# Two layers of cached attention and FFN: most of TensorE's program becomes a repeated block of four units

## The chip, the cores and the metric

The kernel runs on one core of a Trainium2 chip. Its engines are TensorE (PE: matmuls; PEld: its weight loads), VectorE (DVE), ScalarE (ACT), GpSimd (POOL) and SyncE (SP), which here issues every DMA. Sixteen DMA engines move the data. Each engine runs its own program in order and waits on semaphores for the others. The metric is device microseconds of one execution; times are medians of several runs. A trace of one execution, taken by the hardware profiler, gives a profile.

## What is computed

Four rows of x (batch 4, one position, width 512) go twice through an attention layer over a cache of 8192 keys and values and then through a gated FFN:

```python
def _A_ref(x, k_cache, v_cache, wq, wo):      # Hq 32 heads, Hkv 8 groups, Dh 128
    q = (x @ wq).reshape(B, Sq, Hq, Dh).transpose(0, 2, 1, 3)
    scores = einsum("bhqd,bhkd->bhqk", q, repeat(k_cache, 4)) * Dh ** -0.5
    o = einsum("bhqk,bhkd->bhqd", softmax(scores), repeat(v_cache, 4))
    return o.transpose(0, 2, 1, 3).reshape(B, Sq, Hq * Dh) @ wo
def _B_ref(x, w_gate, w_up, w_down):
    return (silu(x @ w_gate) * (x @ w_up)) @ w_down
x = x + _A_ref(_layernorm(x), ...);  x = x + _B_ref(_layernorm(x), ...)   # and both once more
```

Both layers use the same weights and the same caches. K and V are 64 MB each in bf16, read once per layer.

## The kernel before

**Units.** A unit is one pair of a key group g (8) and a batch row b (4): 2 MB of K and 2 MB of V, 32 units a layer. `unit_order` runs through them, in layer 1 beginning with the last three of layer 0, whose K and V are kept in memory and not loaded again. In this text "the 31st unit" is the 31st in a layer's order.

**Slots.** SBUF has eight slots of 2 MB for K and V (`NSLOT`). `pump` (L316) issues loads on SP in a fixed order (`items`: K of a unit, then V of the unit before it, in between and at the end the weights), each into a free slot that `fit` and `max` choose. A load is issued when `finished` (L363) has put a slot back: after the last scores of a K, after the last product of a V. At the end of a layer the weights of the FFN take slots 6 and 7.

**The work of a unit.** DVE transposes each of the eight blocks of a K in place (`turn`, L401). PE computes the scores of a block with four matmuls (`scores`, L421), with the queries that POOL has laid out in `zq` (`place_q`, L412). When all eight are done, the steps of the softmax follow: DVE's maximum over the partitions (`max_p`, L427), PE's transpose of it and DVE's second maximum (`max_t`, L431 and L434), ACT's copy (L437), PE's spreading of it and ACT's exponentials (`exps`, L443, L447, L449, L451), DVE's transpose of the probabilities (`turn_p`, L454), PE's sums and their reciprocal (`total`, L457, L459). Then PE multiplies them with V (`values`, 16 matmuls, L517), ACT and DVE add up the parts (L526, L531), PE sums rows (L536) and DVE scales into `oT` (L556). For the last two units of a layer V is taken in 8 blocks of 8 small matmuls (`block_last`, L549).

**Order.** The program of every engine is written out in full by Python, in one order. DVE's transposes are emitted first; the blocks that use them lag behind by at most `LAG` = 2.0 us of estimated work (`drain`), and the steps of softmax (`line`) and of the sums (`after`) are put between blocks as their estimated gaps run down (`advance`, L382). Each operation waits for what it reads and for the readers of what it writes (`_Sync`); a wait is a constant value of a semaphore. TensorE's program is 9,792 matmuls and weight loads long.

**Projection.** When the four units of a group are done, `out_proj` (L575) multiplies the group's outputs with its part of `wo`: 16 small matmuls that bring `oT` into place (L581), a copy to `o4` on DVE (L584), 16 matmuls (L587) and DVE's addition to x (L572). So there is one after every fourth unit, and `oT` has two buffers.

**Between layers.** `center` (L597 to L610) and `deviation` (L613) are the layer norm, `ffn` (L647) takes gate and up (L659), SiLU (L664 to L671) and down (L676), `qproj` (L621) the queries of the next layer.

## Time and profile before

| what | value |
|---|---|
| runs | 655.31 us median of 3 (654.31 to 655.44) |
| the profiled execution | 655.51 us, its span 653.7 us |
| mean granted TensorE clock | 0.824 |
| HBM read | 273.88 MB, 419 GB/s over the span |
| DVE transposes of K, L401, x488 | 322.4 us, 686 ns each; idle before them 121.8 us, ended by the load of K |
| PE scores, L421, x2048 | 346.2 us, 314 ns each |
| PE products with V, L517, x960 | 68.5 us, 409 ns each |
| PE projections, L581 and L587, x256 each | 6.6 and 9.2 us |
| DVE addition to x, L572, x21 | 3.6 us; idle before it 15.3 us, 11.2 of it for PE's L587 |
| loads of K, x60, and of V, x58, 2 MB | 30.0 and 33.8 us from issue to landing |

The first part of the page gives each engine's busy time and its share of the span. The slices show forty equal parts of the span: a 9 in the DMA row means that the sixteen DMA engines were busy for nine tenths of that slice or more. The rows on queues tell whose packets the DMA engines moved: q1 carries the kernel's loads, q8 and q14 instructions of the engines' programs. The chain is followed back from the last instruction to whatever released each step. A line of a timeline has the start and the length in us, the engine, the line of the program, the operation with what it writes and reads, the count of merged instructions, and in brackets the engine's idle time before and what ended it. Under all this the trace keeps one record for each DMA packet: its queue, size, start and duration. A load ends on each DMA engine with a packet of 4 bytes, the completion mark.

### The profile page before, as it was taken

The numbers are of one execution on the slowest core, as the hardware profiler recorded it, in microseconds if no ns is written. First come the engines' busy times: TensorE is split into PE (matmuls) and PEld (weight loads), VectorE is DVE, ScalarE is ACT, GpSimd is POOL, SyncE is SP. The second block draws the span as 40 slices with busy tenths as digits, with TensorE's granted clock in tenths as the row PEclk, the third lists the DMA queues.
The fourth block names the chain that finished last, engine by engine and source line by source line (L and its number), as shares of the span: only waits on it lengthen the run. The fifth ranks groups of instructions, "written<-read, shape, count | busy, mean of one in ns | idle before, by whom it ended". The sixth has DMA issues, their size and how long they took to land.

```text
span 653.7 us, 11807 instructions
## 1 busy us (share of the span) xinstructions
PE 500.5 (77%) x4896; PEld 319.2 (49%) x4896; DVE 446.1 (68%) x1079; ACT 116.4 (18%) x391; POOL 19.3 (3%) x73
## 2 busy tenths in 40 slices
PE   1766787977777877787876988887688787786886
PEld 1544444544444544544555655554354454443456
DVE  2556676776776777776752399996677677676682
ACT  0021121221221221221220212221122122121120
POOL 0000000000000000000000000000000000000000
PEclk9897788777978778789685989997978887797895
DMA  9999999999999999999999999999999999999996
GB/s 368 428 425 423 438 429 427 432 431 429 430 431 429 430 430 432 430 432 428 427 416 375 398 411 431 430 428 429 430 428 429 433 430 430 432 427 429 432 420 239
DMA packets 24085, 274.64 MB, mean 420 GB/s; under 512 B 2392, under 2 KB 2400, under 8 KB 7904
## 3 DMA queue, kind: packets, MB, share of 16 engines
q1 hardware_dynamic: 24032, 273.89, 98.9%
q8 instruction: 38, 0.62, 0.3%
q14 instruction: 15, 0.12, 0.0%
HBM read 273.88 MB, written 0.00 MB: 419 GB/s over the span
## 4 chain that ended last, share of the span: by engine, by line
DMA 66%; DVE 17%; PE 13%; SPq 3%; issue 1%; ACT 0%; POOL 0%; DVEq 0%; POOLq 0%
DMA kvf<-in_A_k_cache_dram 63%; DVE kvf L401 11%; PE ps L421 8%; DVE acc L531 3%; DMA kvf<-in_B_w_down_dram 3%; SPq L93 2%; PE ps L517 1%; DVE one L427 1%; DVE pT L454 1%; PE ps L587 1%; DVE m L434 1%; PE ps L625 1%; PE ps L457 0%; PE ps L676 0%; PE ps L549 0%
## 5 line engine op out<-in xcount | busy, mean ns | idle before, releaser
L401 DVE STREAM_TRANSPOSE kvf<-kvf 128x512 f32<-128x512 f32 x488 | 322.4, 686 | 121.8 <-DMA kvf<-in_A_k_cache_dram 121.8
L421 PE MATMUL ps<-kvf,zq 128*128 128x256 bf16 x2048 | 346.2, 314 | 18.2 <-DVE kvf L401 15.7
L421 PEld LDWEIGHTS ps<-kvf,zq 128*128 128x128 bf16 x2048 | 211.3, 115 | 89.8 <-DVE kvf L401 40.4
L437 ACT ACTIVATE pb<-m 1x128 f32<-1x128 f32 x64 | 19.7, 308 | 453.5 <-DVE m L434 453.5
L431 PE MATMUL ps<-identf,one 128*1 128x128 f32 x64 | 18.3, 286 | 68.3 <-DVE one L427 68.3
L517 PE MATMUL ps<-kvf,pT 128*16 128x512 bf16 x960 | 68.5, 409 | 0.9 <-DVE rl L459 0.9
L531 DVE SCALAR_TENSOR_TENSOR acc<-ps,own,acc 128x128 f32<-128x128 f32 x180 | 63.1, 351 | 6.5 <-ACT acc L526 1.9
L431 PEld LDWEIGHTS ps<-identf,one 128*1 128x1 f32 x64 | 5.1, 80 | 99.4 <-DVE one L427 93.2
L536 PE MATMUL ps<-head,acc 128*128 128x4 f32 x120 | 26.4, 290 | 17.9 <-DVE acc L531 17.7
L536 PEld LDWEIGHTS ps<-head,acc 128*128 128x128 f32 x120 | 22.8, 237 | 34.2 <-DVE acc L531 33.6
L443 PE MATMUL ps<-one,pb 1*128 1x1 f32 x128 | 27.8, 284 | 14.1 <-ACT pb L437 13.8
L443 PEld LDWEIGHTS ps<-one,pb 1*128 1x128 f32 x128 | 22.4, 217 | 32.8 <-ACT pb L437 29.1
L449 ACT ACTIVATE pb<-ps,one,rstd 128x256 bf16<-128x256 f32 x64 | 36.2, 565 | 2.1
L412 POOL TENSOR_TENSOR zq<-scr,quad 128x64 bf16<-128x64 bf16 x62 | 18.2, 293 | 608.1 <-PE ps L421 569.4
L517 PEld LDWEIGHTS ps<-kvf,pT 128*16 128x16 bf16 x960 | 19.3, 91 | 32.8 <-issue 21.2
L427 DVE TENSOR_REDUCE one<-ps 128x1 f32<-128x256 f32 x64 | 25.6, 399 | 13.1 <-PE ps L421 12.7
L454 DVE STREAM_TRANSPOSE pT<-pb 128x256 bf16<-128x256 bf16 x64 | 25.9, 405 | 1.9 <-ACT pb L449 1.9
L457 PEld LDWEIGHTS ps<-rsm,one 128*128 128x128 f32 x128 | 24.5, 237 | 3.0 <-ACT rsm L451 0.9
L457 PE MATMUL ps<-rsm,one 128*128 128x4 f32 x128 | 21.6, 239 | 0.0
L447 ACT ACTIVATE one<-ps,rstd 128x1 f32<-128x1 f32 x64 | 16.7, 261 | 25.8 <-PE ps L443 25.8
L526 ACT ACTIVATE acc<-ps,own 128x128 f32<-128x128 f32 x60 | 20.6, 343 | 0.0
L434 DVE TENSOR_REDUCE m<-ps 1x4 f32<-1x128 f32 x64 | 15.6, 244 | 6.5 <-PE ps L431 6.5
(66 smaller groups left out, 165.9 us busy)
## 6 DMA issues: line engine op xcount, KB each, us to landing
kvf<-in_A_k_cache_dram SPq DMA_DIRECT2D x60, 2048.0 KB, 30.0
kvf<-in_A_v_cache_dram SPq DMA_DIRECT2D x58, 2048.0 KB, 33.8
wq_sb<-in_A_wq_dram SPq DMA_DIRECT2D x4, 1024.0 KB, 7.6
wo_sb<-in_A_wo_dram SPq DMA_DIRECT2D x4, 1024.0 KB, 34.5
kvf<-in_A_v_cache_dram SPq DMA_DIRECT2D x8, 512.0 KB, 19.3
kvf<-in_B_w_gate_dram SPq DMA_DIRECT2D x2, 1792.0 KB, 23.2
kvf<-in_B_w_down_dram SPq DMA_DIRECT2D x4, 768.0 KB, 16.0
kvf<-in_A_v_cache_dram SPq DMA_DIRECT2D x2, 1024.0 KB, 7.0
```

The lines of the kernel that those rows point to most:

```text
L401: T.op("dve", lambda e: e.transpose(w, w), reads=[f"s{s}.{q}"], writes=[f"s{s}.{q}"])
L421: T.op("pe", lambda e: e.matmul(bank(bk)[:, 0:SW], lhsT=zq[:, c, z0:z0 + P], rhs=w[:, :, c // 2, :, c % 2], start=(q == 0 and c == 0), sto ...
L427: T.op("dve", lambda e: e.tensor_reduce(mx[:], bank(bk)[:, 0:SW], AX.X, ALU.max), reads=[f"pb{bk}"], writes=["mx"])
L431: T.op("pe", lambda e: e.matmul(bank(STEP)[0:1, 0:P], lhsT=mx[:], rhs=identf[:], is_transpose=True, start=True, stop=True), reads=["mx", " ...
L434: T.op("dve", lambda e: e.tensor_reduce(m4[:], bank(STEP)[0:1, 0:P].rearrange("p (x h) -> p h x", h=REP), AX.X, ALU.max, negate=True), rea ...
L443: T.op("pe", lambda e: e.matmul(bank(STEP)[:, 0:1], lhsT=mrow, rhs=onesf[0:1, :], start=True, stop=True), reads=["pb", "onesf"], writes=[f ...
L449: T.op("act", lambda e: e.activation(pb[:], bank(bk)[:, 0:SW], ACTF.Exp, bias=nm[:], scale=by, accum_out=rs[:]), reads=[f"pb{bk}", "nm", " ...
L454: T.op("dve", lambda e: e.transpose(pT[:, turn_of[u], :], pb[:]), reads=["pb"], writes=[f"pT{turn_of[u]}"])
L457: T.op("pe", lambda e: e.matmul(bank(TOT)[:, 0:REP], lhsT=ones, rhs=rsm[:], start=True, stop=True), reads=["rsm", "onesf"], writes=[f"pb{T ...
L517: T.op("pe", lambda e: e.matmul(bank(bk)[j * QB:j * QB + NV * REP, :], lhsT=pT[:, turn_of[u], c0:c0 + NV * REP], rhs=v[:, t, NV * i:NV * ( ...
L531: T.op("dve", lambda e: e.scalar_tensor_tensor(acc[:], bank(bk)[:, k * Dh:(k + 1) * Dh], own[:, k:k + 1], acc[:], op0=ALU.mult, op1=ALU.ad ...
L536: T.op("pe", lambda e: e.matmul(bank(LNB)[:, 0:REP], lhsT=acc[:], rhs=head[:], start=True, stop=True), reads=["acc", "head"], writes=[f"pb ...
```

## The change

- **A tape for TensorE.** Matmuls are no longer issued at once. `T.pe` records them, with their waits, on a tape, and `play` issues them at the end of the build. The other engines' programs are built as before.
- **A repeated block.** `roll` cuts the tape at the heads of the units, looks in each layer for the longest run in which the operations of four units equal those of the next four (but for the values of the semaphores, which must grow by a constant step), and issues four units as the body of a `Fori` on TensorE with the rest of that run left out. The head of the loop is put at slot 0 of an instruction fetch block. In the body a wait's value is computed in a register from the loop's counter.
- **Slots.** `home` gives every load a fixed slot: in layer 0 K takes slots 0 to 3 in turn and V 4 to 7, in layer 1 K 7, 2, 3, 6 and V 5, 0, 4, 1, with exceptions at the ends of the layers. A load waits for its own slot, no longer for any.
- **Projections.** `project` takes several groups at once. Groups 0, 1, 2 are projected ahead of the scores of the 31st unit, groups 3, 4, 5 ahead of those of the 32nd, in layer 0 group 6 there too; the rest at the end as before. Ahead of those scores the copy to `o4` runs on ACT. `oT` has a buffer per group.
- **Small arrays.** `xs` and `lnv` are merged into `vs`; `zq` and `o4` are laid out anew.

```diff
+    def pe(self, out, lhsT, rhs, reads=(), writes=(), sig=True, **kw):
+        left = self._open("pe", self._need(reads, writes))
+        self.tape.append(((out, lhsT, rhs), left, sig, kw))
+        self.count["pe"] += sig
+        self._record("pe", (self.prog["pe"], self.count["pe"] + (not sig)), reads, writes)
+
+    def play(self, ops, value=lambda sem, val: val):
+        e = self.eng["pe"]
+        for (out, lhsT, rhs), left, sig, kw in ops:
+            for sem, val in left:
+                e.wait_ge(sem, value(sem, val))
+            ins = e.matmul(out, lhsT=lhsT, rhs=rhs, **kw)
+            if sig:
+                ins.then_inc(self.prog["pe"], 1)
...
-        zq = sb("zq", [P, 4, ZP + P], BF16)
+        zq = sb("zq", [P, ZP + 4 * P], BF16)
...
-        free = list(range(NSLOT))
+        free = set(range(NSLOT))
+        CYCLE = NSLOT // 2
+        def home(it):
+            kind, L, u = it
+            i = unit_order[L].index(u)
+            if L == 0:
+                return i % CYCLE if kind == "K" else {NU - 2: 0, NU - 1: CYCLE}.get(i, CYCLE + i % CYCLE)
+            if kind == "K":
+                return 0 if i == NU - 1 else (7, 2, 3, 6)[i % CYCLE]
+            return {NU - 3: 1, NU - 2: 4, NU - 1: 5}.get(i, (5, 0, 4, 1)[i % CYCLE])
...
-                late = any(e - 10 < n < e for e in ends)
-                fit = [s for s in free if s < NKEEP or not late]
-                if not fit:
+                s = home(it)
+                if s not in free:
                     return
-                s = fit[0] if late else max(fit, key=lambda s: s >= NKEEP)
...
         def keys(L, u):
             def block(q):
                 first = u == unit_order[L][0]
+                if q == 0:
+                    tails.append(len(T.tape))
+                    at = L, unit_order[L].index(u)
+                    for gs in between.get(at, ()):
+                        project(gs, "act")
+                    heads.append(len(T.tape))
                 if q == 0 and not first:
                     place_q(u)
...
+        between = {(0, NU - 2): [[0, 1, 2]], (0, NU - 1): [[3, 4, 5], [6]],
+                   (1, NU - 2): [[0, 1, 2]], (1, NU - 1): [[3, 4, 5]]}
+        late_g = {(L, g) for L in range(2) for g in range(G)}
+        late_g -= {(L, g) for (L, _), lists in between.items() for gs in lists for g in gs}
...
-            if all((L, g * B + k) in done for k in range(B)):
-                rest.append([0.5, None, lambda: out_proj(g)])
+            if (L, g) in late_g and all((L, g * B + k) in done for k in range(B)):
+                rest.append([0.5, None, lambda: project([g], "dve")])
...
-        def out_proj(g):
+        def project(gs, eng):
+            n = len(gs)
             pick = ident.rearrange("p (j e) -> p e j", e=REP)
-            ob = bank(OUTB)[:, XB:2 * XB].rearrange("p (e b) -> p e b", b=B)
+            ob = bank(OUTB)[:, XB:XB + REP * n * B]
+            grid = ob.rearrange("p (e g b) -> p e g b", e=REP, b=B)
             for c in range(REP):
                 for h in range(REP):
...
+                    T.pe(grid[h * QB:(h + 1) * QB, c, :, :], pick[:, c, :], oT[:, gs[0]:gs[0] + n, h, :],
+                         reads=[f"oT{g}" for g in gs] + ["ident"], writes=[f"pb{OUTB}"], sig=(h == REP - 1),
+                         start=True, stop=True)
+            if eng == "dve":
+                T.op("dve", lambda e: e.tensor_copy(o4[:, 0:REP * n * B], ob), reads=[f"pb{OUTB}"], writes=["o4"])
+            else:
+                T.op("act", lambda e: e.activation(o4[:, 0:REP * n * B], ob, ACTF.Copy), reads=[f"pb{OUTB}"], writes=["o4"])
+            to = [(c, k) for k in range(n) for c in range(REP)]
             for nt in range(KT):
...
+                for c, k in to:
+                    T.pe(bank(OUTB)[:, nt * B:(nt + 1) * B], wo_sb[:, gs[k], c, nt * P:(nt + 1) * P],
+                         o4[:, (c * n + k) * B:(c * n + k + 1) * B],
...
             add_to_x()
...
+        def roll():
+            ops = T.tape
+            part = [ops[a:b] for a, b in zip(heads, tails[1:] + [len(ops)])]
+            said = [[(repr(aps), [id(w[0]) for w in left], sig, kw) for aps, left, sig, kw in seg] for seg in part]
...
+            at = 0
+            pe = mybir.EngineType.PE
+            for L in range(2):
+                run = {}
+                for n in range(L * NU + 1, L * NU + NU - CYCLE - 1):
+                    m = n
+                    while m + CYCLE < L * NU + NU - 1 and said[m] == said[m + CYCLE] and strides(m) and \
+                            strides(m) == strides(n + (m - n) % CYCLE):
+                        m += 1
+                    run[n] = m - n
+                n = max(run, key=run.get)
+                turns = run[n] // CYCLE + 1
...
+                T.play(ops[at:heads[n]])
+                with nc.Fori(1, 1 + turns, 1, engines=(pe,), head_slot={pe: 0}) as i:
+                    T.play(body, lambda sem_, v: nc.tensor.to_reg(i * step[id(sem_)] + (v - step[id(sem_)])))
+                at = tails[n + CYCLE * turns]
+            T.play(ops[at:])
```

## The prediction

> **What bounds the kernel now.** I read the page's share of busy time and its slices first, then the DMA queues and the chain, then the timeline at the end of each layer.

> ```profile
> span 653.7 us, 11807 instructions
> ...
> PE 500.5 (77%) x4896; PEld 319.2 (49%) x4896; DVE 446.1 (68%) x1079; ACT 116.4 (18%) x391; POOL 19.3 (3%) x73
> ...
> DMA  9999999999999999999999999999999999999996
> ...
> q8 instruction: 38, 0.62, 0.3%
> ...
> DMA 66%; DVE 17%; PE 13%; SPq 3%; issue 1%; ACT 0%; POOL 0%; DVEq 0%; POOLq 0%
> ```

> The DMA row is full until the last slice: the kernel streams 274.64 MB at 420 GB/s, and most work hides under that. In the steady part a 2 MB load occupies an engine for 4.86 us (the trace's packet records), so a unit (one K, one V) takes 9.72 us. PE is busy 142.12 of the 180 us from 120 to 300, 7.7 us a unit, and has 2.0 us to spare; loads land 30.0 and 33.8 us after issue, so some 25 us of transfers are queued ahead and a short stall of PE starves nothing.

> Near the end of each layer this cover goes. Layer 0 ends in waits for transfers (first PE's timeline), while in layer 1 DVE and PE have no idle time behind the last K (then DVE's):

> ```profile
> 341.36 0.59 PE L600 MATMUL ps<-xs,one 128*128 128x4 f32 x2 [0.48 <-DVE xs L598]
> 342.89 0.91 PE L659 MATMUL ps<-xn,kvf 128*128 128x4 bf16 x28 [0.94 <-DMA kvf<-in_B_w_gate_dram]
> ...
> 347.31 1.63 PE L659 MATMUL ps<-xn,kvf 128*128 128x4 bf16 x56 [2.34 <-DMA kvf<-in_B_w_up_dram]
> 349.25 0.80 PE L676 MATMUL ps<-scr,kvf 128*128 128x4 bf16 x24 [0.31 <-DVE scr L671]
> 351.04 1.07 PE L676 MATMUL ps<-scr,kvf 128*128 128x4 bf16 x32 [0.98 <-DMA kvf<-in_B_w_down_dram]
> ```

> ```profile
> 620.35 0.71 DVE L401 STREAM_TRANSPOSE kvf<-kvf 128x512 f32<-128x512 f32 x1 [2.49 <-DMA kvf<-in_A_k_cache_dram]
> ...
> 622.67 0.69 DVE L401 STREAM_TRANSPOSE kvf<-kvf 128x512 f32<-128x512 f32 x1
> 623.37 1.12 DVE L531 SCALAR_TENSOR_TENSOR acc<-ps,own,acc 128x128 f32<-128x128 f32 x3
> 624.41 1.29 DVE L401 STREAM_TRANSPOSE kvf<-kvf 128x512 f32<-128x512 f32 x2
> ...
> 630.57 0.24 DVE L434 TENSOR_REDUCE m<-ps 1x4 f32<-1x128 f32 x1
> 630.74 1.88 DVE L401 STREAM_TRANSPOSE kvf<-kvf 128x512 f32<-128x512 f32 x3
> ```

> The reader sees three DMA waits in the first (0.94 + 2.34 + 0.98 = 4.3 us) that could absorb a late PE. In the second there is none behind 620.35: the last 33.3 us of the span are computing, started by the landing of the 31st unit's K.

> **Fetches: a gain.** 38 packets times 256 is 9,728, TensorE's 9,792 matmuls and weight loads: q8 is its program, one packet of 16 KB per 256 instructions, some 20 us apart. The share of 0.3% hides what it does. In the packet records each fetch sits on one DMA engine and takes 0.88 to 0.97 us; that engine's next completion marks come 1.41 to 1.42 us late and stay late, because its queue never runs empty, while the other fifteen go on. Successive fetches go round eight engines. A load is done when its slowest engine is. So the K of layer 0's 31st unit is done on the first engine at 313.82 and on the last at 317.62 (DVE starts at 317.97); that of layer 1's 31st unit at 615.15 and 619.93.

> A unit has 32 + 16 + 1 + 2 + 2 + 2 = 55 matmuls (L421, L517, L431, L443, L457, L536), four units 440 instructions; two blocks hold 512. If the block stays in TensorE's instruction memory, a turn fetches nothing. About 4 fetches ahead of the loop and 2 for its body then precede the K of layer 0 in place of 15, at most one per engine: skew 0.6 (start) + 1.42 + up to 0.55 (a fetch of another engine) = 2.6 in place of 3.8 us, a gain of 1.2 to 1.8; I take 1.5. Layer 1's engines start again nearly level (1.15 us between first and last at 376 to 377); with one fetch each, 1.15 + 1.42 = 2.6 in place of 4.8: gain 2.2, at least 1.4 and at most 2.8 (one or two fetches).

> [...] No run here shows a branch.

> **Register arithmetic and the branch: nothing.** Four units leave at most 512 - 440 = 72 other instructions, 18 a unit, at 15 ns (L676: 56 matmuls and their loads in 1.65 us) to 51 ns (TensorE's 82 waiting instructions in the trace): 0.3 to 0.9 us a unit, under the 2.0 to spare. The back edge is not in the trace; up to 4 x 2.0 = 8 us a turn it would be hidden too, and below zero it can't be. I take nothing for both. When layer 1 catches up (366 to 412) a unit takes 7.05 us (391.21 to 398.26 between issues of K), still under 9.72 with 0.9 added.

> **Slots: nothing.** Followed through by hand, the new homes issue nearly every load at the same finished unit as before. The fifth K waits for the first (six loads are ahead of it); near layer 1's end one V is issued one unit later, at 612.5, with V, K and K (about 12 us) still ahead of it, and the last V and the weights half a unit later, at 619. All under cover; if it went, a gap would cost that part of 9.7 us.

> **Projections moved: a loss.** Six of eight groups leave the stream, where they were hidden, and stand ahead of the scores of the 31st and 32nd unit. A batch of three costs PE 16 matmuls, 0.42 us (L581's row), then a copy on ACT, 0.26 (L447, the nearest), then 48 matmuls, 0.14 + 48 x 0.028 = 1.49 (L549: 28 ns each). DVE's add waits for all of it, and DVE's transposes are queued behind.

> Layer 1: PE reaches the batch at 621.70 (behind L431) and ends the first part at 622.12; ACT is behind L437 and L526 until 623.33; copy to 623.59; matmuls to 625.13; add to 625.35. DVE was free at 623.36: 2.0 us late. Scores that ran from 621.54 start at 625.1. The second batch stands behind the 31st unit's last scores and stops DVE for 0.9 more; L434 of 630.57 comes 2.9 late, and L443, behind PE's scores, 3.3 late. I laid all instructions from there on out in program order with these durations; without the change the layout ends 0.7 us from the trace, with it 3.3 us later. Lower end: PE is idle 13.70 - 10.24 = 3.5 us from 620.3 to 634; if the 2 x 1.91 us filled all of that, 0.4 us. Upper end: 2 x (1.91 + ACT's 1.5) = 6.8.

> Layer 0 adds the seventh group (0.42 + 0.26 + 0.59, behind the add of the batch before): the same layout gives 4.9 us. Less the earlier K (1.5) and the waits that absorb it (4.3), layer 0 ends 0.9 us earlier; bounds -1.5 (the weights' own gain) to +2.

> **Sum.** -0.9 (layer 0's end) - 2.2 (fetches of layer 1) + 3.3 (batches in layer 1) = +0.2 us. The profiled run took 655.51 us, 1.8 more than its span and 0.2 over the median; on the median 655.31 I forecast **655.5 us**: no change, two parts cancelling. A difference under 0.2%, 1.3 us, is about what a measurement of this kernel can't tell from none.

> **Rivals.**
> - *The loop's head is fetched again each turn* (slower, and the change doesn't do what it says). Two blocks a turn are what the plain program fetches, three if the block behind the loop is drawn too. With two no lag is gained: layer 0's end 4.9 - 4.3 = +0.6, layer 1 +3.3, so 659.2. With three, six turns add at most one fetch per engine and layer: 2 x 1.42 more, 662.0. It decides once a turn fetches two blocks. For it: each block was fetched when the one before began. Against: eight engines in turn look like room for more than two blocks. Price 660. [...]
> - *The batches are hidden* (faster): PE's 3.5 us of idle time takes up nearly all, 1.0 us is left, and the lag falls by two fetches: -1.5 - 2.8 + 1.0 = -3.3, 652.0. Against: the add stops DVE, which has no idle time there.
> - *PE becomes the bound*: registers at over 111 ns each (2.0 / 18), say 0.14, cost 18 x 0.14 = 2.5 a unit, 0.5 over what is free, on 48 units 24 us: 679. No row is near that price.

> **How the numbers follow.** Forecast 0.45 (of it 0.21 within 0.2%, 0.14 slower, 0.10 faster, as the batches and the lag err by 1 to 2 us each); refetch 0.29; hidden 0.22; PE 0.04. So faster 0.32, same 0.21, slower 0.47. The forecast's own range is 653.5 to 657.5. The range, 651.5 to 661.5, takes in the hidden batches and most of the refetch, and leaves out PE as the bound, and the outer tails.

> **What would show it.** q8 at some 20 packets (right) or 38 and more (refetch). DVE's start on layer 1's 31st K some 3 us earlier, and the time from there to the end 33.3 + 3.3 us. New idle time of DVE ahead of the add of each batch (the line that answers to L572), waiting for PE. The three DMA waits at layer 0's end shrunk or gone. Loads still landing 25 us or more after issue in the steady part. The forecast is wrong if the end moves with neither.

## The result and the profile after

The changed kernel takes 657.91 us, median of 8 runs (656.32 to 660.51); the kernel before, run beside it, 655.12 (654.31 to 655.68, 8 runs). The ratio is 1.0042, 95% interval 1.0028 to 1.0055: slower by 0.4%, where no change, 655.5, was forecast. The runs lie 4.2 us apart, those of before 1.4. The profiled run took 657.03 us, a span of 655.0. From its page come the span, TensorE's row, the DMA row of the slices, TensorE's program queue and the chain's shares by engine:

```profile
span 655.0 us, 12103 instructions
...
PE 493.9 (75%) x4768; PEld 320.3 (49%) x4768; DVE 441.1 (67%) x1058; ACT 117.2 (18%) x396; POOL 19.3 (3%) x73
...
DMA  8999999999999999999997999999999999999995
...
q8 instruction: 19, 0.31, 0.2%
...
DMA 66%; PE 17%; DVE 14%; SPq 1%; issue 1%; ACT 1%; POOL 0%; DVEq 0%; POOLq 0%
```

TensorE's program is fetched 19 times in place of 38, and in the packet records none of these falls between 69 and 322 us or between 414 and 615: the body stays. But the DMA row, full before, now has a 7 in the middle, at the end of layer 0, and PE's share of the chain went from 13% to 17%. Two timelines show where. First PE at the end of layer 0 (start, duration, and in brackets the idle time ahead and what ended it), then SP's queue there:

```profile
346.03 0.59 PE L96 MATMUL ps<-vs,one 128*128 128x4 f32 x2 [0.48 <-DVE vs L636]
346.98 0.89 PE L96 MATMUL ps<-xn,kvf 128*128 128x4 bf16 x28 [0.36 <-DVE acc L644]
...
348.16 2.38 PE L96 MATMUL ps<-xn,kvf 128*128 128x4 bf16 x84
350.97 1.66 PE L96 MATMUL ps<-scr,kvf 128*128 128x4 bf16 x56 [0.43 <-DVE scr L704]
```

```profile
350.61 2.37 SPq L114 DMA_DIRECT2D kvf<-in_A_k_cache_dram  x2
```

The same line of the kernel before:

```profile
349.02 3.44 SPq L93 DMA_DIRECT2D kvf<-in_A_k_cache_dram  x2
```

The three waits for weights are gone, as forecast: PE is now later than the weights. But the last of the gate and up matmuls ends at 348.16 + 2.38 = 350.54, and the first K of layer 1, whose room the weights hold, is issued right behind it, at 350.61; before it was 349.02. By then the queue of transfers has run dry: the DMA engines are busy 18% of 348 to 350 us, in the kernel before 65%. Now layer 1's tail, DVE and then PE:

```profile
619.23 0.71 DVE L428 STREAM_TRANSPOSE kvf<-kvf 128x512 f32<-128x512 f32 x1 [2.71 <-DMA kvf<-in_A_k_cache_dram]
...
623.74 0.17 DVE L604 TENSOR_TENSOR xT<-xT,ps 128x16 f32<-128x16 f32 x1 [1.51 <-PE ps L96]
...
631.63 0.17 DVE L604 TENSOR_TENSOR xT<-xT,ps 128x16 f32<-128x16 f32 x1 [0.68 <-PE ps L96]
```

```profile
620.50 0.42 PE L96 MATMUL ps<-oT,identf 128*32 128x12 bf16 x16
622.35 1.35 PE L96 MATMUL ps<-o,wo_sb 128*128 128x4 bf16 x48 [1.43 <-ACT o L621]
```

DVE stands idle ahead of both adds, 1.51 and 0.68 us, and PE waits 1.43 for the copy on ACT. From DVE's start on the 31st K to the end of the span it is 655.0 - 619.23 = 35.8 us, before 653.7 - 620.35 = 33.4. The start itself is 1.1 us earlier, where the prediction had some 3.

### The profile page after: what moved, and what is told of

Read it like the earlier page. It is cut to its first block, busy times and chain, and to the rows that moved or that the text cites. A ratio compares the mean times of both kernels' runs of the same rounds, so it can differ in the third digit from the quotient of the medians.

```text
span 655.0 us, 12103 instructions
## 1 busy us (share of the span) xinstructions
PE 493.9 (75%) x4768; PEld 320.3 (49%) x4768; DVE 441.1 (67%) x1058; ACT 117.2 (18%) x396; POOL 19.3 (3%) x73
## 4 chain that ended last, share of the span: by engine, by line
DMA 66%; PE 17%; DVE 14%; SPq 1%; issue 1%; ACT 1%; POOL 0%; DVEq 0%; POOLq 0%
DMA kvf<-in_A_k_cache_dram 66%; PE ps L96 17%; DVE kvf L428 8%; DVE acc L564 2%; SPq L114 1%; DVE one L454 1%; DVE m L460 0%; DVE pT L479 0%; ACT pb L463 0%; ACT acc L559 0%; DVE xT L604 0%; DVE scr L702 0%; ACT o L621 0%; DVE oT L589 0%; DVE scr L679 0%
## 5 line engine op out<-in xcount | busy, mean ns | idle before, releaser
L96 PE MATMUL ps<-kvf,pT 128*16 128x512 bf16 x960 | 64.2, 389 | 0.7 <-DVE rl L484 0.7
L96 PEld LDWEIGHTS ps<-one,pb 1*128 1x128 f32 x128 | 23.6, 229 | 35.8 <-DVE m L460 28.5
L472 ACT ACTIVATE one<-ps,rstd 128x1 f32<-128x1 f32 x64 | 16.7, 261 | 36.9 <-PE ps L96 36.9
L476 ACT ACTIVATE rsm<-head,one 128x4 f32<-128x4 f32 x64 | 19.0, 298 | 2.1
```

What stands on the lines that cost most here:

```text
L96: ins = e.matmul(out, lhsT=lhsT, rhs=rhs, **kw)
L472: T.op("act", lambda e: e.activation(nm[:], bank(STEP)[:, 0:1], ACTF.Copy, scale=by), reads=[f"pb{STEP}", "rstd"], writes=["nm"])
L476: T.op("act", lambda e: e.activation(rsm[:], head[:], ACTF.Copy, scale=rs[:]), reads=["head", "rs"], writes=["rsm"])
```

## The experiments

All times are medians, with a ratio to the kernel before on the same chip. "Batches" are the projections of several groups; "late" is where the change has them (ahead of the 31st and 32nd unit's scores); "early" is ahead of the 28th, 29th and 30th unit's. The rows come from three chips; the kernel before took 655.14 to 655.25 us beside them.

| kernel | us (range, runs) | ratio, 95% interval | fetches |
|---|---|---|---|
| slots alone | 655.34 (654.42 to 656.60, 12) | 0.9999, 0.9988 to 1.0010 | 38 |
| late batches, no loop | 659.06 (658.05 to 661.27, 6) | 1.0063, 1.0043 to 1.0083 | 37 |
| the changed kernel again | 658.73 (656.24 to 661.07, 7) | 1.0061, 1.0039 to 1.0082 | 19 |
| early batches, loop | 653.65 (652.80 to 654.35, 12) | 0.9971, 0.9960 to 0.9983 | 23 |
| early batches, no loop | 655.65 (654.50 to 656.74, 12) | 1.0002, 0.9992 to 1.0013 | 37 |
| late in layer 0 only, loop | 653.75 (652.89 to 658.12, 12) | 0.9982, 0.9967 to 0.9996 | 21 |
| the same again | 653.89 (653.12 to 657.15, 12) | 0.9984, 0.9971 to 0.9997 | 21 |
| late in layer 1 only, loop | 656.41 (655.41 to 656.96, 12) | 1.0013, 1.0004 to 1.0022 | 21 |
| changed, adds deferred | 658.42 (656.23 to 661.66, 12) | 1.0049, 1.0031 to 1.0068 | 19 |
| late in layer 1 only, copy on DVE | 658.70 (656.79 to 660.34, 6) | 1.0056, 1.0040 to 1.0072 | 21 |
| changed, six turns | 657.36 (657.05 to 661.22, 6) | 1.0049, 1.0030 to 1.0068 | 23 |
| six turns, matmuls added | 658.81 (656.80 to 660.95, 6) | 1.0054, 1.0037 to 1.0070 | 23 |

**The slots alone.** The tape is played straight through and every group is projected when it is done:

```diff
         def roll():
+            T.play(T.tape)
...
-        between = {(0, NU - 2): [[0, 1, 2]], (0, NU - 1): [[3, 4, 5], [6]],
-                   (1, NU - 2): [[0, 1, 2]], (1, NU - 1): [[3, 4, 5]]}
+        between = {}
```

> The new slots and small arrays alone: no loop, and each group's projection where it stood before. My theory (slots cost nothing): 655.1 us like before, within 0.6, about 38 fetches, K of layer 1's 31st unit done some 4.8 us after its first engine, and the end 33.4 us behind DVE's start on it. Rival (the fixed slots delay loads): 656.5 or more, with the loss in layer 1 ahead of the 31st K. Rival (chance of which engine is fetched for): anything up to 2 us off, with the same issue order.

655.34 us, as before: the slots and small arrays cost nothing. One expectation failed, and it matters for reading single profiles: with the same 38 fetches layer 1's 31st K is done 3.6 us after its first engine, not 4.8, and DVE starts on it at 618.88 in place of 620.35. The fetches fall at other moments in the two profiles, so a start in one profile is uncertain by some 1.5 us.

**The change without the loop, and the changed kernel again.** The first has the edit of `roll` alone, the second none.

> The change without the loop: new slots, batches of projections at the layers' ends, TensorE's program in full. Theory (the loop takes fetches away and gains 1.0 to 1.6 us in layer 1, the batches lose about 2.4 there and 0.5 in layer 0): 659.0 to 659.6 us, 37 or 38 fetches, the K of layer 1's 31st unit done 4.8 us after its first engine. Rival (the loop itself costs, by its entry, its registers or its back edge): under 657.5, faster than the changed kernel. Rival (batches are free): 655.

> The changed kernel again, for its scatter and a second profile. Theory (the batches stand in the path at both ends): 657.9 us, runs from 656.3 to 660.5, in the profile 35.8 us from DVE's start on layer 1's 31st K to the end, give or take TensorE's granted clock there. Rival (the 4.2 us of scatter came from one bad spell): median below 656.5.

Without the loop it is 659.06, so the loop does not cost what was lost; it gains 0.3 to 1.2 us (against 658.73 and 657.91), less than expected and not clear of the intervals. The changed kernel repeats: slower, and its scatter with it.

**The batches moved ahead,** where a unit is bound by its transfers, with the loop and without. The search for the loop's body ends with the first batch, which costs a turn per layer:

```diff
-        between = {(0, NU - 2): [[0, 1, 2]], (0, NU - 1): [[3, 4, 5], [6]],
-                   (1, NU - 2): [[0, 1, 2]], (1, NU - 1): [[3, 4, 5]]}
+        between = {(L, NU - 5 + k): [gs] for L in range(2) for k, gs in enumerate(([0, 1, 2], [3, 4], [5]))}
...
-                    while m + CYCLE < L * NU + NU - 1 and said[m] == said[m + CYCLE] and strides(m) and \
+                    while m + CYCLE < L * NU + NU - 5 and said[m] == said[m + CYCLE] and strides(m) and \
```

> The change with the batches moved ahead of the layers' last units: groups 0 to 2 ahead of the 28th unit's scores, 3 and 4 ahead of the 29th's, 5 ahead of the 30th's, the others one by one as before; the loop has one turn fewer per layer. Theory (the batches lose at the ends and nothing where PE has 2 us a unit to spare; the loop gains 1 to 1.6): 653.3 to 654.5 us, about 24 fetches, 33.4 us from DVE's start on layer 1's 31st K to the end. Rival (the loop costs, not the batches): 657 to 658 as the changed kernel.

> The batches moved ahead (as in the kernel with the loop and early batches, 653.65 us), without the loop. Theory (each fetch takes 1.42 us from one of sixteen DMA engines, so 15 fetches fewer give 15 x 1.42 / 16 = 1.3 us of stream): 654.7 to 655.3 us, 37 or 38 fetches, the bytes moved by 612 us about 1.3 us behind those of the kernel with the loop. Rival (the loop gains nothing and the larger batches alone gained 1.5 us, by fewer matmuls): 653.7.

653.65 us with the loop: faster than both kernels, by 0.3% than the one before, with runs 1.6 us apart. Without it 655.65, as before, a little over the 655.3 expected. So with early batches the loop is worth 2.0 us, and the batches' places make the whole of the loss. The packet records give the loop's part as stream: by 612 us the kernel without the loop has moved 0.2 us less of data than the kernel before (bytes, at 431 GB/s), that with it 1.1 us more. The difference of 1.3 is about that of 14 fetches of 1.42 us, each on one of sixteen engines, 14 x 1.42 / 16 = 1.2. The other 0.7 us of the medians is not resolved by the stream. The two profiles, 655.73 and 654.17 us, show where to look: DVE starts on layer 1's 31st K 0.5 us later without the loop (619.38, 618.84), and 1.0 us more is lost behind it, in the last FFN. First PE without the loop, then with it:

```profile
644.58 0.91 PE L96 MATMUL ps<-xn,kvf 128*128 128x4 bf16 x28 [0.68 <-DMA kvf<-in_B_w_gate_dram]
...
650.82 0.16 PE L96 MATMUL ps<-scr,kvf 128*128 128x4 bf16 x1 [0.43 <-issue]
```

```profile
643.79 0.89 PE L96 MATMUL ps<-xn,kvf 128*128 128x4 bf16 x28 [0.36 <-DVE acc L643]
...
647.78 1.65 PE L96 MATMUL ps<-scr,kvf 128*128 128x4 bf16 x56 [0.43 <-DVE scr L703]
```

Without the loop PE waits for weights there and stops ahead of its last matmul of this product. These are single profiles; that fetches cause both stops is not shown.

**Late in one layer only.** The places of the change in one layer, the early ones in the other (shown for layer 0; for layer 1 the two are exchanged); the loop's search ends at each layer's first batch. The one with layer 0 ran twice.

```diff
-        between = {(0, NU - 2): [[0, 1, 2]], (0, NU - 1): [[3, 4, 5], [6]],
-                   (1, NU - 2): [[0, 1, 2]], (1, NU - 1): [[3, 4, 5]]}
+        between = {(0, NU - 2): [[0, 1, 2]], (0, NU - 1): [[3, 4, 5], [6]]} | {(1, NU - 5 + k): [gs] for k, gs in enumerate(([0, 1, 2], [3, 4], [5]))}
...
+                stop = min(i for l, i in between if l == L)
...
-                    while m + CYCLE < L * NU + NU - 1 and said[m] == said[m + CYCLE] and strides(m) and \
+                    while m + CYCLE < L * NU + stop and said[m] == said[m + CYCLE] and strides(m) and \
```

> The changed kernel with the late batches in layer 0 alone; in layer 1 they are early. Theory (in layer 0 they free the slots late, and layer 1's first loads are issued 1.6 us late): 654.8 to 655.6 us, 1.2 to 1.9 above the kernel with all batches early (653.65). Rival (the queue of loads takes layer 0's delay up, all the loss is in layer 1's tail): 653.7.

> The changed kernel with the late batches in layer 1 alone; in layer 0 they are early. Theory (2.4 to 3.3 us in layer 1's tail): 656.1 to 657.0 us, 35.8 to 36.9 us from DVE's start on layer 1's 31st K to the end, where the kernel with all batches early has 33.6. Rival (all loss is here): 658.0 or more. Rival (it comes from layer 0): 653.7.

> Late batches in layer 0 alone, once more. Theory (late batches in layer 0 make a gap in the stream of 0.6 to 4 us by the granted clock, of which some is made up): median 653.7 to 655.0, single runs up to 658. Rival (the first 12 runs' 658.12 was a stray, layer 0's batches are free): median 653.5 to 653.9, none above 655.5.

Late batches in layer 1 cost 656.41 - 653.65 = 2.8 us, as expected, with little scatter. In layer 0 they cost 0.1 to 0.2 at the median, where 1.2 to 1.9 was expected, but 4 of 24 runs lie 2.5 to 4.4 us above the median. The two profiled runs happen to be one of each, 652.89 and 656.39 us. Six stretches of the layer's end (us; PE, PEld, DVE, ACT and POOL busy; granted clock, the share of full speed at which TensorE's clock ran; DMA share; GB/s) were read in both and in the kernel with early batches. Three of the six are shown; first the shorter run with late batches, then the longer, then the early one:

```profile
324.00:330.00 6.00, 5.68 (x86) 4.60 (x85) 5.45 (x12) 1.13 (x4) 0.29 (x1) 0.75 0.98 416
330.00:336.00 6.00, 5.36 (x79) 4.34 (x77) 3.62 (x9) 1.71 (x6) 0.00 (x0) 1.00 1.01 410
...
348.00:354.00 6.00, 4.31 (x129) 3.81 (x126) 2.68 (x15) 0.08 (x1) 0.00 (x0) 0.50 0.71 238
```

```profile
324.00:330.00 6.00, 5.69 (x47) 4.37 (x46) 4.74 (x12) 1.43 (x5) 0.29 (x1) 0.65 0.97 409
330.00:336.00 6.00, 5.35 (x95) 4.18 (x96) 2.68 (x8) 0.49 (x2) 0.00 (x0) 0.63 1.02 412
...
348.00:354.00 6.00, 5.21 (x158) 5.07 (x159) 2.34 (x11) 0.81 (x3) 0.00 (x0) 0.50 0.26 63
```

```profile
324.00:330.00 6.00, 4.64 (x38) 3.07 (x37) 6.00 (x14) 1.26 (x5) 0.29 (x1) 1.00 0.99 424
330.00:336.00 6.00, 5.55 (x115) 4.06 (x113) 3.09 (x11) 2.03 (x7) 0.00 (x0) 0.95 1.01 413
...
348.00:354.00 6.00, 3.30 (x90) 2.87 (x90) 1.84 (x12) 0.00 (x0) 0.00 (x0) 0.50 0.92 341
```

With late batches PE is busy 5.4 to 5.7 of 6 us from 324 to 336: it sets the layer's end. In the longer run its granted clock there is 0.63 to 0.65, the eight score matmuls behind the last batch take 1.87 us in place of 1.05, layer 1's first K is issued at 352.51 in place of 349.31, and the DMA engines are busy 26% of 348 to 354 in place of 71%. The scores and the issue, in the shorter run and then in the longer:

```profile
331.73 1.05 PE L96 MATMUL ps<-kvf,zq 128*128 128x256 bf16 x8
...
349.31 2.24 SPq L114 DMA_DIRECT2D kvf<-in_A_k_cache_dram  x2
```

```profile
332.85 1.87 PE L96 MATMUL ps<-kvf,zq 128*128 128x256 bf16 x8
...
352.51 2.37 SPq L114 DMA_DIRECT2D kvf<-in_A_k_cache_dram  x2
```

That gap is the whole difference: bytes moved by 612 us stand 3.4 us apart, the run times 3.5.

The same reading of ten profiles (time at the granted clock of 0.5 summed over sixteen stretches from 318 to 340 us, and what the stream loses against the kernel before between 345 and 355 us):

| late batches in layer 0? | kernel | us at half clock | stream lost, us |
|---|---|---|---|
| no | early, loop | 4.6 | -0.2 |
| no | late in layer 1 only | 4.9 | -0.3 |
| yes | late in layer 0 only | 3.4 | 1.2 |
| yes | changed, again | 3.4 | 1.4 |
| yes | changed, six turns | 6.8 | 1.4 |
| yes | changed | 6.8 | 2.6 |
| yes | no loop | 10.2 | 1.6 |
| yes | late in layer 0 only, again | 13.7 | 4.3 |
| yes | six turns, matmuls added | 13.9 | 4.0 |
| yes | changed, adds deferred | 13.7 | 4.5 |

The other four profiles have no late batches in layer 0; they have 4.7 to 4.9 us at half clock and lose nothing either. Without late batches the slow clock costs nothing there, since PE waits for weights (2.34 us for one of them before, 2.42 with early batches and the loop). With late batches it goes with the loss, two profiles (no loop and changed) less well than the others.

**The adds deferred.** Each batch's sum stays in its own columns until the next single projection, so no transpose is queued behind its add.

```diff
+            at = 0
+            if eng == "act":
+                at = 64 + 16 * len(owed)
+                owed.append(at)
+            else:
+                while owed:
+                    add_to_x(at=owed.pop(0))
...
-                    T.pe(bank(OUTB)[:, nt * B:(nt + 1) * B], wo_sb[:, gs[k], c, nt * P:(nt + 1) * P],
+                    T.pe(bank(OUTB)[:, at + nt * B:at + (nt + 1) * B], wo_sb[:, gs[k], c, nt * P:(nt + 1) * P],
...
-            add_to_x()
+            if eng == "dve":
+                add_to_x()
```

> The changed kernel with its batches of projections where they are, but each batch's sum kept in its own columns and added to x by DVE only ahead of the next projection that comes one by one, so DVE's transposes of the last two K don't wait behind the add. Theory (DVE's stop at the add is what the batch costs, as the prediction had it): 655.8 to 656.6 us, no idle time of DVE ahead of the adds in the tail. Rival (the scores behind the batch on TensorE are late whatever DVE does): 657.8 or more.

658.42 us: nothing gained, as the rival had it. DVE's timeline in layer 1's tail shows why:

```profile
624.74 1.12 DVE L565 SCALAR_TENSOR_TENSOR acc<-ps,own,acc 128x128 f32<-128x128 f32 x3
625.78 1.29 DVE L428 STREAM_TRANSPOSE kvf<-kvf 128x512 f32<-128x512 f32 x2
629.74 0.17 DVE L590 TENSOR_TENSOR oT<-ps,rl 128x4 bf16<-128x4 f32 x1 [2.67 <-PE ps L96]
```

The stop of 1.51 at the add is gone, and DVE waits 2.67 us for PE two steps later. Part of the 2.67 is the clock: the eight scores behind the batch take 1.87 us in this profile and 1.05 in that of the change. The kernel with late batches in layer 1 only, whose eight scores take 1.87 too, has both stops, 1.53 + 1.01 = 2.54 us together:

```profile
622.45 0.17 DVE L603 TENSOR_TENSOR xT<-xT,ps 128x16 f32<-128x16 f32 x1 [1.53 <-PE ps L96]
...
625.88 0.17 DVE L588 TENSOR_TENSOR oT<-ps,rl 128x4 bf16<-128x4 f32 x1 [1.01 <-PE ps L96]
```

So the wait only moved. DVE's stop was a symptom. PE carries the batch, its wait for the copy and the scores one after the other.

**The copy on DVE.** The kernel with late batches in layer 1 only, with one word changed:

```diff
-                        project(gs, "act")
+                        project(gs, "dve" if L == 1 else "act")
```

> Late batches in layer 1 alone (656.41 us with the copy to o4 on ACT), with that copy on DVE in layer 1. Theory (TensorE waits 1.43 us for the copy since ACT is behind the maxima's row and the scaling of the unit before; on DVE it stands behind a transpose or two): TensorE's wait ahead of the first batch's second part 0.3 to 0.9 us, 655.5 to 656.2. Rival (the matmuls of the batch and the stop of DVE make the price, the copy's engine doesn't matter or DVE is the dearer): 656.4 or more.

Dearer: 658.70, as the rival had it. PE waits as long for DVE, which has transposes in front, and at the second batch longer than for ACT (0.31):

```profile
621.06 1.35 PE L96 MATMUL ps<-o,wo_sb 128*128 128x4 bf16 x48 [1.46 <-DVE o L618]
...
629.97 1.35 PE L96 MATMUL ps<-o,wo_sb 128*128 128x4 bf16 x48 [1.38 <-DVE o L618]
```

The profiled run, 656.96 us, is one of the two shortest of six and no longer than the one with the copy on ACT, 656.85. What makes the other four 1 to 3.4 us longer is in no trace here.

**Six turns, and six turns with PE kept busy.** The first has the shorter search of the early kernels and the change's batches; the second adds matmuls:

```diff
+        pb2 = wq_sb[:, 0, 0:256]
...
         def max_t(u):
+            i = unit_order[L].index(u)
+            for _ in range({NU - 5: 10, NU - 4: 10, NU - 3: 4}.get(i, 0)):
+                T.pe(bank(OUTB)[:, 256:512], ident, pb2, writes=["spare"], sig=False, start=True, stop=True)
```

> The changed kernel with its batches where they are, but six turns of the loop per layer in place of seven, as the kernels with early batches have them. Theory (the batches' places alone make the loss; the loop's length matters little, one turn is 2 fetches): 657.6 to 658.9 us, 23 fetches, like the changed kernel's 657.9 and 658.7. Rival (the loop's exit and the fetches behind it, right ahead of each layer's end, cost TensorE there; then late batches in one layer and early ones in the other, which have six turns in one layer at least, showed too little): under 657.2, near the sum of the two halves, 653.65 + 0.1 + 2.8 = 656.5.

> The same as with six turns, and 10, 10 and 4 matmuls of 128x128 by 128x256 that nobody reads, on columns of the bank that nothing else uses, ahead of the turned maxima of each layer's 28th, 29th and 30th unit, where TensorE waits some 2 us for DVE. They compute nothing of the output. Theory (with the late batches TensorE sets the layers' ends, and the granted clock of 0.5 that follows its idle time makes the scores there 1.87 us in place of 1.05, by chance of the phase): granted clock near 1.0 from 300 to 335 us, median 656.0 to 657.2 and the runs within 2.5 us of each other. Rival (the scatter has another cause, or the added matmuls only delay): 658 or more, runs 4 to 5 us apart.

657.36 with six turns: a little under what was expected, not as low as the rival's 657.2, with two of six runs at 659.09 and 661.22. The loop's length explains at most a small part. The added matmuls missed: 658.81, the runs 4.2 us apart, and the clock from 324 to 336 at 0.63 and 0.66. They stand ahead of the batch; the idle time that this profile shows next to the slow clock is inside it, where PE waits 1.2 us for the copy (1.5 in the other seven with late batches in layer 0). In the eight profiles with late batches in layer 0 PE is busy 3.7 to 4.8 us from 318 to 324 and the clock of the next 6 us is 0.63 to 0.82; in the six without PE is busy 5.2 to 6.0 and the next clock is 1.00. The trace's own record of the clock says the same: it falls to 0.5 between 319.3 and 323.8 us in all eight, and in none of the six between 313 and 335. That the wait brings the slow clock is therefore likely but not shown: filling that wait itself was not tried.

## Why the prediction was right or wrong, point by point

The time, 657.91 us, lies in the range of 651.5 to 661.5, which was drawn that wide to take in two rivals, and just outside the forecast's own 653.5 to 657.5; that the wide range holds it says little for the sum. Two parts were to cancel: the loss by the batches came near its forecast, the gain from fetches did not.

- **The sum.** +0.2 was forecast, the medians say +2.8 and, in the repetition, +3.6. Without its gain from fetches the forecast was 0.6 at layer 0's end (4.9 of batches less 4.3 of waits) and 3.3 in layer 1, +3.9; the kernel without the loop took 659.06 - 655.14 = 3.9 us more than before. The gain from fetches was to be 1.5 + 2.2 = 3.7; with late batches it was 0.3 to 1.2, with early ones 2.0. The fetches became as few as forecast; the term that failed is what they were worth. That 3.9 agrees so well is in part luck: the prediction's 0.6 in layer 0 was lateness of the layer's end, and what the runs show there is transfers lost behind it (below).
- **Refetch** (rival): fell. 19 fetches, as "some 20" had it. The time alone would not have told: this rival's lower price was 659.2. The trace of the changed kernel shows that both blocks of the body stay: the back edge was taken six times a layer at 207 to 237 ns, with no fetch from 69 to 322 us nor from 414 to 615.
- **Registers and branch: nothing; slots: nothing.** Right. 566 register operations of 32 ns and 45 of 37, and the catch-up of layer 1 still has 7.05 us a unit; the slots alone run at 655.34.
- **The gain from fetches, layer 1: 2.2 us.** Too large. The early pair gives 2.0 at the medians for both layers together, of which 1.3 shows in the packet records. DVE was to start on layer 1's 31st K some 3 us earlier; in the two profiles of the changed kernel it starts 1.1 and 1.8 earlier (619.23 and 618.57, before 620.35), and the slots alone, with all 38 fetches, have 1.5. The mechanism was put too narrowly: what the records show is that the mean stream is ahead by about 1/16 of each delay (1.3 us for 14 fetches of 1.42); how far the slowest engine is behind the first at this K differs from profile to profile (4.8 us in the kernel before, 3.6 with the slots alone, both with 38 fetches).
- **The gain from fetches, layer 0: 1.5 us.** This term failed. DVE starts on that K at 317.84 (317.97 before): 0.1. Other engines' fetches of 8 KB were counted as "up to 0.55" once; three of them, 78.6 us apart (121.7, 200.3 and 279.0 us), come on the same DMA engine and delay it by some 0.84 us each time. They are DVE's by their period: it runs 129 instructions in 78.6 us, and 8 KB hold 128 if 16 KB hold 256. That engine is the slowest once TensorE's fetches are gone: its completion mark for this K comes 1.45 us behind the last but one.
- **Layer 0 ends 0.9 us earlier.** Failed by that term: 4.9 of batches less 4.3 of waits less 0.1 gives 0.5 later, and the profile has the next layer's start 0.5 later (353.17 in place of 352.65). The prediction's waits did absorb what it said; what it left out is what stands behind them. The first K of layer 1 waits for the gate and up matmuls, so lateness beyond the cover empties the DMA queue: 1.2 to 4.5 us of stream, some of it made up later.
- **Batches in layer 1: +3.3 us.** Right in size: 2.8 at the medians, 2.4 in the profile; over the eight profiles with late batches there the time from the 31st K to the end is 35.7 to 37.3 us, mean 36.6, against 33.1 to 34.6, mean 33.7, without: 2.9. The path was right in part: the layout had PE's scores late too, but the price was put on DVE stopped at the add, and the deferred add shows that PE's own order carries it.
- **"The batches are hidden"** (rival): fell for layer 1, and holds for layer 0 in most runs.
- **What stays open.** The parts measured alone, -2.0, +2.8 and +0.1 to +0.2, give 1.0, and the step from there to the changed kernel, 1.8 to 2.6 us, is not in any part. Some of it is arithmetic: medians of runs with a few long ones don't add. By means late batches cost 0.7 us in layer 0 (24 runs), 2.7 in layer 1, and 4.8 in both (15 runs): 1.3 are left over, not far from the noise of runs that lie 4.8 us apart. Without the loop they cost 3.6 in both by means, 0.1 over the sum of the two. The longer runs are commoner with late batches in both layers (5 of 15 above 659). The clock goes with them, and why it falls more often there stays open.

## What to carry to other kernels

Work moved from a stretch where an engine has spare time to the end of a stage, where that engine sets the end, costs most of its length: here 2.8 us for 2 x 1.8 us of matmuls, with waits of 1.4 and 0.3 us for a copy. Put it where the transfers still bind; the loop lost one turn in seven by that and the kernel became 0.3% faster than before. And when lateness is set against waits that can absorb it, follow one step further: which loads are issued behind that work, and how much the queue still holds then.
